# Rank counts, PSUM copies and planner constants of a fused attention and expert kernel

## Chip, cores and metric

One core of a Trainium2 chip runs the whole kernel in one launch. The metric is the time of the execution in device microseconds; the runs shown are medians, and lower is better. The profiled execution is one more execution of the same program.

## The reference, cut to what matters

Capped attention for 8 batches, 12 heads, 448 positions and 64 features per head, then a mixture of 8 experts over all 3,584 tokens, where each expert keeps the 80 tokens with the largest gate weight:

```python
scores = cap * np.tanh((q @ k.T / 8) / cap)
attn = softmax(scores)
x = (attn @ v)                                   # 3584 tokens x 768
logits = x @ w_gate                              # 3584 x 8
expert_idx = argmax(logits, axis=1)
gate_w = softmax(logits)[arange, expert_idx]
for e in range(8):
    tok_idx = tokens of expert e, at most 80, largest gate_w first
    h = relu(x[tok_idx] @ w1[e])                 # 768 -> 1024
    out[tok_idx] = gate_w[tok_idx] * (h @ w2[e]) # 1024 -> 768
```

## The kernel before, in words

**Two stages on one queue of TensorE.** The attention stage runs from the start to about 413 us, the expert stage from there to the end. Everything is float32 and laid out on each engine in an order written by hand.

**The attention stage** goes over 48 pairs of heads (six to a batch), numbered t. One step t issues, in an order written out in the loop at L1341, letters for pieces of work: `q0` to `q3` (products of queries and keys for pair t, each followed by ScalarE's tanh), `x` and `y` (ScalarE's exponentials of pair t and of pair t-1), `a0` to `a2` and `a3` (products of the exponentials with the values for pair t-2), `r` and `s` (GpSimd's partial sums), `u` (on odd t: TensorE sums the exponentials, `SUMS(u)` below, and VectorE transposes and inverts the sums), `n` and `m` (VectorE scales the two products of one pair of pairs, `x(u,0)` and `x(u,1)`, and transposes them). Even t run `q0 q1 y m a0 a1 b q2 q3 s r b x a2 b u`, odd t run `q0 q1 y a0 b q2 q3 a3 u n b x a1 a2 b`. GpSimd adds up the exponentials (L1103, L1105).

After `SUMS(u)` VectorE has a fixed piece of work: `st` (L1124, a transposition of the sums out of PSUM), reciprocals, `r`, the product `x(u,0)` (L1148), its transposition, and the same for the second half. `x(u,0)` has to be done before `a0` of the next even step may write its PSUM bank again, `x(u,1)` before `a0` of the odd step after it.

**The places.** The letter `b` is a place where other work is put in. There are three in a step; below, 24.1 is the second place of step 24. At each, `background` (L1263) takes pieces from three lists: `urgent` (the routing arithmetic of a batch that is just finished), `low` (fetching rows) and `bg` (the ranking). A piece is a cost in nanoseconds, a function that issues its instructions, and a gap: a piece with gap g goes no earlier than g places after the piece taken last from the same list. A place takes pieces until their costs pass a quota, and each cost is added to a planned clock of VectorE that moves on by `PLACE` = 2,630 ns at each place. From step 33 (`LATER`) a piece also has to end within `SLACK` of that clock, a number by parity of t and place. So costs, gaps and slack alone set the order of the instructions on every queue.

**What a batch b brings.** When its six pairs are done (steps 8, 14, ... 44, and the end for b = 7) `gate` queues: `product` (logits into PSUM, `lgp`, L1180), `kept` (the logits copied to SBUF, `lgs`, L1192), `turn` (TensorE transposes them, `lt`, L1199), `math` and the key (some 20 small instructions of VectorE, which end in the sort key `kc`, L327), and `later`, which puts the ranking of the batch's 448 tokens into `bg`: `ranks` (L396). Batches 0 to 4 form the first table, batches 5 to 7 are ranked with its kept entries.

**Ranking.** `row` transposes the keys into PSUM (`psk`) and copies them to SBUF as one row (`krow`); `ties` compares them with themselves (four small tests, L418); `before(c)` compares the whole row so far with the keys of column c (L439, passes of up to 896 columns); `after(c)` lets TensorE count those comparisons (`pd`, L446); `add(c)` adds the counts to `dfc` (L454). Two columns are compared ahead of the count of the first.

**The first table.** After batch 4 `prune` (L544) works out the kept tokens: `order` (o0 to o5 below), `ranked`, `places`, `parts`, `left` (three passes, L586), `right`, `kept`, then `put`, a product of 20 small matmuls (`prt`, L602), and `keys` from it. Its rows are fetched from DRAM ahead of the expert stage.

**PSUM.** All the small results (`sp` of the sums, `psk`, `lgp`, `lt`, `pd`, `prt`) share two banks under the tag `misc`.

**The expert stage** multiplies six tables of 80 rows with their experts' weights (L798); its queue of TensorE follows that of attention, with two chunks started in step 48. The ranking of the last batch goes on beside it.

Of the kernel before, what the change touches and what calls it, by code (L numbers as in the profile page):

```python
# [12 lines left out]
ALU = mybir.AluOpType  # L13
# [4 lines left out]
B, H, S, D = 8, 12, 448, 64  # L18
NP = H // 2
NQ = H // 4  # L20
C = 112
# [3 lines left out]
NC = S // C  # L25
# [11 lines left out]
OB = 5  # L37
# [15 lines left out]
FLIGHT = 5  # L53
PLACE = 2630
LATER = OB * NP + 3
SLACK = ((6500, 6000, 4500), (3000, 6500, 7500))
LATE = 3
RMB = 34
NBUF = 5
# [56 lines left out]
def attn_moe(ctx, tc, q2, k, v, cap, wg, w1, w2, capacity, ct, out):  # L116
    nc = tc.nc
# [25 lines left out]
    def cst(key, n=128):  # L143
        a, b = CT[key]
        return ctt[:n, a:b]
# [15 lines left out]
    acc = consts.tile([C, OCOL, NACC], F32, name="acc")  # L161
# [234 lines left out]
    def ranks(krow, gp, pl, tag, b, acc, dfc, x0, c0, blocks, gw=GW, end=None, ahead_=False):  # L396


        nb = b * NC - c0
        nk = len(blocks)  # L400
        starts = blocks + [x0 + i * C for i in range(nb + NC)]
        PW = PCOL * C

        def row():
            psk = pl.tile([128, 512], F32, name=f"psk{b}", tag=tag, bufs=2)
            for c in range(NC):
                nc.tensor.transpose(psk[:C, c * C:(c + 1) * C], kc[:, b * NC + c:b * NC + c + 1].broadcast_to([C, C]), cst("ident", C)[:, :C])
            z["row"] = nc.scalar.copy(krow[:, x0 + nb * C:x0 + (nb + NC) * C], psk[:C, :S])
            z["psk"] = psk
            held[0] += ahead_  # L410

        gs, z = {}, {}

        def ties():
            held[0] -= 1
            for i, (c, kp, _) in enumerate(cols):
                g = gp.tile([C, C], BF16, name=f"gl{b}_{c}", tag="gl")
                d = nc.vector.scalar_tensor_tensor(g, z["psk"][:C, i * C:(i + 1) * C], kp, cst("tri", C), op0=ALU.is_equal,  # L418
                                                   op1=ALU.mult, accum_out=acc[:, nk + c, 1:2])
                if i == 0:  # L420
                    tc.add_manual_dep(d.ins, z["row"].ins.name, flight, reason="row")

        def tied(c, kp):
            g = gp.tile([C, C], BF16, name=f"gl{b}_{c}", tag="gl")
            x = x0 + c * C
            nc.vector.scalar_tensor_tensor(g, krow[:, x:x + C], kp, cst("tri", C), op0=ALU.is_equal,
                                           op1=ALU.mult, accum_out=acc[:, nk + c, 1:2])

        def before(c, i, x, y, kp, act=False):
            if c not in gs:  # L430
                gs[c] = gp.tile([C, gw], BF16, name=f"gb{b}_{c}", tag="gb", bufs=LATE)
            g, a = gs[c][:, x:y], acc[:, nk + c, 2 + i:3 + i]
            if act:
                nc.vector.tensor_scalar(g, krow[:, x:y], kp, None, op0=ALU.is_ge)
                z = sm.tile([CK, 2, S], F32, name=f"gz{b}_{c}", tag="t1", bufs=4)
                z = z.rearrange("p a b -> p (a b)").bitcast(BF16)[:C, x:y]
                nc.scalar.activation(z, g, AF.Copy, accum_out=a)
            else:
                nc.vector.tensor_scalar(g, krow[:, x:y], kp, 0.0, op0=ALU.is_ge, op1=ALU.add, accum_out=a)  # L439

        def after(c):
            g = gs.pop(c)
            n = nk + c
            pd = pl.tile([128, 512], F32, name=f"pd{b}_{c}", tag=tag, bufs=2)
            for i in range(n):
                nc.tensor.matmul(pd[:, i:i + 1], g[:, starts[i]:starts[i] + 128], ones_b[:, 0:1], start=(i == 0), stop=(i == n - 1))  # L446
            pds[c] = pd[:C, :n]
            held[0] += 1

        def add(c):  # L450
            pd = pds.pop(c)
            held[0] -= 1
            n = pd.shape[-1]
            nc.vector.tensor_tensor(dfc[:, :n], dfc[:, :n], pd, op=ALU.add)  # L454
        pds = {}
        yield 300, row, 2
        cols = [(c, kc[:, c0 + c:c0 + c + 1], x0 + (c + 1) * C) for c in range(nb, nb + NC)]
        if end is not None:
            x = x0 + nb * C

            def first(i):
                c, kp, _ = cols[i]
                return 1700, lambda: before(c, 0, 0, x, kp), 0

            def second(i):
                c, kp, m = cols[i]
                yield 400, lambda: before(c, 1, x, m, kp), 0
                yield 400, lambda: tied(c, kp), 0
            for i in range(LATE):
                yield first(i)  # L470
            for i in range(0, NC, 2):
                yield from second(i)
                yield from second(i + 1)
                yield 100, lambda i=i: after(nb + i), 2
                yield 100, lambda i=i: after(nb + i + 1), 0
                if i == 0:
                    yield first(LATE)
                    yield 200, lambda: add(nb), 0
                    yield 200, lambda: add(nb + 1), 0
                else:  # L480
                    yield 200, lambda i=i: add(nb + i), 1
            yield 800, lambda: end(pds.pop(nb + NC - 1)), 0
            return
        late = []
        gap = 1
        if ahead_:
            yield 1500, ties, 1
            gap = 0
        for c, kp, m in cols:
            for i in range((m + PW - 1) // PW):  # L490
                x, y = i * PW, min(m, (i + 1) * PW)
                yield (y - x) * 1.2 + 120, lambda c=c, i=i, x=x, y=y, kp=kp: before(c, i, x, y, kp), gap
                gap = 0
            if not ahead_:
                yield 400, lambda c=c, kp=kp: tied(c, kp), 0
            if nk + c:
                late.append(c)
            if len(late) == LATE - 1:
                c_ = late.pop(0)
                yield 200, lambda c=c_: after(c), 0  # L500
                yield 200, lambda c=c_: add(c), 1
        for i, c in enumerate(late):
            yield 200, lambda c=c: after(c), int(i == 0)
        for i, c in enumerate(late):
            yield 200, lambda c=c: add(c), int(i == 0)
# [38 lines left out]
    def prune(krow, sm, pl, tag):  # L544

        z = {}
# [122 lines left out]
        for i in range((OCOL + 11) // 12):  # L669
            yield 1000 if i == 0 else 500, lambda i=i: right(i), 0  # L670
        yield 1000, kept, 0
        yield 300, put, 1
        yield 1000, keys, 1
        yield 700, early, 0
        yield 900, rows_in, 0
# [88 lines left out]
    flight = mybir.DependencyInfo(mybir.DependencyClass.Sync, mybir.DependencyReason.DATA)  # L764
# [235 lines left out]
    krow = kr.tile([C, max(OCOL * C, CAND + WCOL * C)], F32, name="krow")  # L1000
# [3 lines left out]
    urgent = []  # L1004
# [6 lines left out]
    st = {"laid": set()}  # L1011
# [4 lines left out]
    with ExitStack() as a2:  # L1016
# [165 lines left out]
        def gate(b):  # L1182
# [6 lines left out]

            def kept():  # L1190
                held[0] -= 1
                nc.scalar.copy(st["lgs", b], st["lp", b][0:96, :S])  # L1192

            def turn():
                lg = st["lgs", b]
# [51 lines left out]
            st["wait"]()  # L1247
            urgent.append((300, product, 0 if b < OB else 1))
            if b < B - 1:
                urgent.append((100, kept, 1))  # L1250
            urgent.append((300, turn, 1 if b < B - 1 else 2))
            urgent.append((1900, lambda: (math(), st["math"][0]()), 1 if b < OB else "ordered"))
            if b < B - 1:
# [9 lines left out]
        def background(quota, took=PLACE, slack=1e9):  # L1263

            now[0] += 1
            clock[0] += took
            for q, last in ((urgent, 1), (low, 3), (bg, 2)):  # L1270
                while q and quota > 0:
                    cost, f, gap = q[0]
                    if gap == "end":
                        if not st.get("end") and quota < 1e8:
                            break
                        gap = 0
                    if gap == "ordered":
                        if not st.get("ordered"):
                            break
                        gap = 1  # L1280
                    if quota < 1e8:
                        if now[0] < now[last] + gap or (gap and slack < 1e8 and clock[0] < ready_at[last]):
                            break
                        if max(clock) + cost > clock[0] + slack:
                            return
                    q.pop(0)
                    quota -= cost
                    vector(cost)
                    now[last] = now[0]
                    ready_at[last] = clock[1]  # L1290
                    f()
# [33 lines left out]
        for t in range(n + 2):  # L1325
# [12 lines left out]
            if 1:  # L1338
# [3 lines left out]
                for i, x in enumerate(todo):  # L1342
# [26 lines left out]
                    elif k_ == 'b' and t < n + 2:  # L1369
                        share = sum(c for c, _, _ in bg + urgent) / (3 * (left - 1) + todo[i:].count('b'))  # L1370
                        share += sum(c for c, _, _ in low) / max(1, 3 * (n - 2 - t))
                        background(min(max(share, 600), 2200 if t < LATER else 3000 if t < n else 4500), PLACE, SLACK[t % 2][todo[:i].count('b')] if LATER <= t < n - 1 else 1e9)
                    if k_ == "b" and t == n + 1 and todo[:i].count("b") == 1:
# [140 lines left out]
```

## Time and profile before

| | us |
|---|---|
| median of 3 runs (lowest, highest) | 529.76 (528.90, 529.96) |
| the profiled execution | 529.38 |
| its span, first to last instruction | 527.2 |
| outside the span | 2.2 |
| attention, 0 to 413.5: TensorE busy, granted clock | 374.3, 0.97 |
| experts, 413.5 to 527.2: TensorE busy, granted clock | 93.9, 0.97 |

A row of the profile names the line, the engine (PE is TensorE, PEld its weight loads, DVE VectorE, ACT ScalarE, POOL GpSimd), the tile written and the tiles read, the shape, a count, and in brackets the idle time ahead of the instruction with what ended it. The granted clock is the share of full speed that TensorE was given: 1.00 is 2.4 GHz and 0.50 is 1.2 GHz.

### The profile page before, as it was taken

The numbers are of one execution on the slowest core, as the hardware profiler recorded it, in microseconds if no ns is written. First come the engines' busy times: TensorE is split into PE (matmuls) and PEld (weight loads), VectorE is DVE, ScalarE is ACT, GpSimd is POOL, SyncE is SP. The second block draws the span as 40 slices with busy tenths as digits, with TensorE's granted clock in tenths as the row PEclk, the third lists the DMA queues.
The fourth block names the chain that finished last, engine by engine and source line by source line (L and its number), as shares of the span: only waits on it lengthen the run. The fifth ranks groups of instructions, "written<-read, shape, count | busy, mean of one in ns | idle before, by whom it ended". The sixth has DMA issues, their size and how long they took to land.

```text
span 527.2 us, 12171 instructions
## 1 busy us (share of the span) xinstructions
PE 468.2 (89%) x4708; PEld 217.0 (41%) x4708; DVE 274.2 (52%) x875; ACT 323.7 (61%) x326; POOL 318.8 (60%) x243
## 2 busy tenths in 40 slices
PE   6799999799999989989999799959978888788894
PEld 2232232223333333323333233323333687787894
DVE  1044435445663585667468955994667835141200
ACT  4988879578888877887888569818850102101111
POOL 0788897587998787799778444624593025325101
PEclk9999999899999999999999899969997999989998
DMA  4675286465576384476674289836356599999901
GB/s 122 193 224 136 67 202 162 119 171 132 146 240 147 77 241 108 107 200 188 137 198 131 67 224 262 204 94 157 80 189 256 170 357 375 387 371 384 360 18 45
DMA packets 82354, 98.15 MB, mean 186 GB/s; under 512 B 37904, under 2 KB 67376, under 8 KB 82288
## 3 DMA queue, kind: packets, MB, share of 16 engines
q1 hardware_dynamic: 80304, 92.66, 60.1%
q0 software_dynamic: 1984, 4.63, 2.7%
q8 instruction: 39, 0.64, 0.5%
q14 instruction: 27, 0.22, 0.1%
HBM read 73.75 MB, written 23.51 MB: 184 GB/s over the span
## 4 chain that ended last, share of the span: by engine, by line
PE 65%; ACT 14%; DVE 13%; issue 6%; DMA 1%; SPq 0%; POOL 0%; POOLq 0%; ACTq 0%; DVEq 0%
PE sc L1061 17%; PE av L1086 13%; PE yt L798 8%; ACT e L1069 8%; PE hp L798 7%; ACT e L1074 5%; PE sp L1119 5%; PE sc L1068 4%; PE av L1095 3%; PE lgp L1180 3%; DVE r L1141 2%; DVE gb L439 2%; PE pd L446 2%; DVE x L1148 2%; DVE rd L1140 1%
## 5 line engine op out<-in xcount | busy, mean ns | idle before, releaser
L1069 ACT ACTIVATE e<-sc,scl 128x896 f32<-128x896 f32 x168 | 162.2, 1014 | 76.6 <-PE sc L1061 70.3
L1074 ACT ACTIVATE e<-e,capt 128x1792 f32<-128x1792 f32 x96 | 154.6, 1611 | 0.0
L1061 PE MATMUL sc<-qt,kt 64*128 64x448 f32 x576 | 140.1, 588 | 10.7 <-ACT e L1069 6.0
L1105 POOL TENSOR_TENSOR t<-t,e 128x896 f32<-128x896 f32 x48 | 100.4, 2092 | 72.1 <-ACT e L1074 70.7
L1086 PE MATMUL av<-e,vr 128*64 128x448 f32 x576 | 134.7, 576 | 2.8 <-issue 2.8
L1103 POOL TENSOR_TENSOR t<-e 128x896 f32<-128x896 f32 x48 | 101.3, 2110 | 34.2 <-ACT e L1074 29.8
L1061 PEld LDWEIGHTS sc<-qt,kt 64*128 64x128 f32 x576 | 49.9, 191 | 83.9 <-ACT e L1069 36.5
L1112 POOL TENSOR_TENSOR t<-t,e 64x448 f32<-64x448 f32 x68 | 76.2, 1130 | 2.6
L1124 DVE STREAM_TRANSPOSE st<-sp 128x448 f32<-128x448 f32 x24 | 15.6, 649 | 110.5 <-PE sp L1119 91.9
L1086 PEld LDWEIGHTS av<-e,vr 128*64 128x64 f32 x576 | 34.3, 139 | 85.2 <-issue 69.9
L439 DVE TENSOR_SCALAR_CACHE_REDUCE gb<-krow,kc 112x896 bf16<-112x896 f32 (+16 forms) x59 | 53.2, 931 | 8.9 <-PE pd L446 8.9
L798 PE MATMUL yt<-thv,w 128*64 128x80 f32 x1152 | 45.1, 238 | 9.7 <-issue 9.7
L798 PEld LDWEIGHTS yt<-thv,w 128*64 128x64 f32 x1152 | 42.9, 141 | 11.2 <-issue 11.1
L798 PE MATMUL hp<-xt,w 128*64 128x80 f32 x1152 | 43.8, 234 | 1.9 <-issue 1.8
L798 PEld LDWEIGHTS hp<-xt,w 128*64 128x64 f32 x1152 | 41.5, 137 | 4.3 <-issue 4.0
L842 POOL DMA_INDIRECT out_dram<-ysv,si x6 | 5.7, 956 | 44.1 <-ACT ysv L841 38.4
L1141 DVE STREAM_TRANSPOSE r<-rd 128x448 f32<-128x448 f32 x48 | 31.0, 645 | 1.7
L1156 DVE STREAM_TRANSPOSE xb<-x 128x448 f32<-128x448 f32 x48 | 30.8, 644 | 1.6
L1148 DVE TENSOR_TENSOR x<-av,r 128x448 f32<-128x448 f32 x48 | 29.8, 620 | 2.1 <-DVE r L1141 0.5
L1119 PE MATMUL sp<-t,ones 128*32 128x448 f32 x192 | 27.9, 568 | 0.8 <-DVE dfc L454 0.8
L814 ACT COPY ty0v<-yt 128x240 f32<-128x240 f32 x6 | 2.2, 359 | 37.6 <-PE yt L798 37.6
L446 PE MATMUL pd<-ones_b,gb 112*128 112x1 bf16 x352 | 13.6, 164 | 12.4 <-DVE gb L439 9.4
(223 smaller groups left out, 341.9 us busy)
## 6 DMA issues: line engine op xcount, KB each, us to landing
w<-in_w_dram SPq DMA_DIRECT2D x36, 512.0 KB, 6.1
w<-in_w_dram SPq DMA_DIRECT2D x48, 384.0 KB, 6.1
kt<-in_k_dram SPq DMA_DIRECT2D x96, 112.0 KB, 2.7
qt<-in_q_dram SPq DMA_DIRECT2D x96, 112.0 KB, 2.9
xs<-xb SPq DMA_DIRECT2D x56, 168.0 KB, 3.5
vr<-in_v_dram SPq DMA_DIRECT2D x24, 256.0 KB, 3.4
out_dram<-zero SPq DMA_DIRECT2D x4, 1536.0 KB, 7.2
vr<-in_v_dram SPq DMA_DIRECT2D x24, 192.0 KB, 3.0
```

What stands on the lines that cost most here:

```text
L439: nc.vector.tensor_scalar(g, krow[:, x:y], kp, 0.0, op0=ALU.is_ge, op1=ALU.add, accum_out=a)
L798: nc.tensor.matmul(ps[j // per][64 * h:64 * h + 64, j % per * m:(j % per + 1) * m], w[:, 128 * j + 64 * h:128 * j + 64 * h + 64], x[:, xk, ...
L1061: nc.tensor.matmul(ps[:, h, :S], s["k"][w, x:x + CK], s["q"][w], start=True, stop=True)
L1069: nc.scalar.activation(s["e"][:, 2 * c:2 * c + 2], ps[:, :, :S], AF.Tanh, scale=scl)
L1074: nc.scalar.activation(x, x, AF.Exp, scale=capt)
L1086: nc.tensor.matmul(st["av", u, f][64 * h:64 * h + 64, :S], st[p]["v"][:, h, c], st[p]["e"][:, 2 * c + h], start=(c == 0), stop=(c == NK - ...
L1103: nc.gpsimd.tensor_tensor(t1, e[:, 0:2], e[:, 2:4], op=ALU.add)
L1105: nc.gpsimd.tensor_tensor(s["es"], s["es"], e[:, 4:6], op=ALU.add)
L1112: nc.gpsimd.tensor_tensor(t1[w, h], t1[w, h], late(p)[w], op=ALU.add)
L1119: nc.tensor.matmul(sp[32 * i:32 * i + 32, :S], ones[:, 0:32], s["es"][:, g % 2, :], start=True, stop=2 * u < RMB)
L1141: nc.vector.transpose(r.rearrange("p (a b) -> p a b", b=32), rd.rearrange("p (a b) -> p a b", b=1).broadcast_to([128, NB, 32]))
L1148: nc.vector.tensor_tensor(x, st["av", u, f][:, :S], st["r", u, f], op=ALU.mult)
```

## The change

Five edits. The copy `krow` of the keys' row is issued by VectorE, at the head of `ties`, where it was ScalarE's in `row` (batch 7 keeps ScalarE's). The copy `lgs` of the logits is VectorE's for batches 0 to 6. `after(c)` gets gap 1 for batches 0 to 3 (gap 0 stays for 4 to 6). `put` gets gap 2. And the planner's numbers change: all six slacks are 1,000 ns larger; a comparison is entered at 1.05 ns a column and 100 ns (1.2 and 120 before), a count at 100 ns (200), `ties` at 1,900 ns (1,500), `kept` at 700 ns (100).

```diff
--- before.py
+++ after.py
@@ -53,7 +53,7 @@
 FLIGHT = 5
 PLACE = 2630
 LATER = OB * NP + 3
-SLACK = ((6500, 6000, 4500), (3000, 6500, 7500))
+SLACK = ((7500, 7000, 5500), (4000, 7500, 8500))
 LATE = 3
 RMB = 34
 NBUF = 5
@@ -405,20 +405,20 @@
             psk = pl.tile([128, 512], F32, name=f"psk{b}", tag=tag, bufs=2)
             for c in range(NC):
                 nc.tensor.transpose(psk[:C, c * C:(c + 1) * C], kc[:, b * NC + c:b * NC + c + 1].broadcast_to([C, C]), cst("ident", C)[:, :C])
-            z["row"] = nc.scalar.copy(krow[:, x0 + nb * C:x0 + (nb + NC) * C], psk[:C, :S])
             z["psk"] = psk
+            if not ahead_:
+                nc.scalar.copy(krow[:, x0 + nb * C:x0 + (nb + NC) * C], psk[:C, :S])
             held[0] += ahead_
 
         gs, z = {}, {}
 
         def ties():
             held[0] -= 1
+            nc.vector.tensor_copy(krow[:, x0 + nb * C:x0 + (nb + NC) * C], z["psk"][:C, :S])
             for i, (c, kp, _) in enumerate(cols):
                 g = gp.tile([C, C], BF16, name=f"gl{b}_{c}", tag="gl")
-                d = nc.vector.scalar_tensor_tensor(g, z["psk"][:C, i * C:(i + 1) * C], kp, cst("tri", C), op0=ALU.is_equal,
-                                                   op1=ALU.mult, accum_out=acc[:, nk + c, 1:2])
-                if i == 0:
-                    tc.add_manual_dep(d.ins, z["row"].ins.name, flight, reason="row")
+                nc.vector.scalar_tensor_tensor(g, z["psk"][:C, i * C:(i + 1) * C], kp, cst("tri", C), op0=ALU.is_equal,
+                                               op1=ALU.mult, accum_out=acc[:, nk + c, 1:2])
 
         def tied(c, kp):
             g = gp.tile([C, C], BF16, name=f"gl{b}_{c}", tag="gl")
@@ -484,12 +484,12 @@
         late = []
         gap = 1
         if ahead_:
-            yield 1500, ties, 1
+            yield 1900, ties, 1
             gap = 0
         for c, kp, m in cols:
             for i in range((m + PW - 1) // PW):
                 x, y = i * PW, min(m, (i + 1) * PW)
-                yield (y - x) * 1.2 + 120, lambda c=c, i=i, x=x, y=y, kp=kp: before(c, i, x, y, kp), gap
+                yield (y - x) * 1.05 + 100, lambda c=c, i=i, x=x, y=y, kp=kp: before(c, i, x, y, kp), gap
                 gap = 0
             if not ahead_:
                 yield 400, lambda c=c, kp=kp: tied(c, kp), 0
@@ -497,7 +497,7 @@
                 late.append(c)
             if len(late) == LATE - 1:
                 c_ = late.pop(0)
-                yield 200, lambda c=c_: after(c), 0
+                yield 100, lambda c=c_: after(c), int(b < OB - 1)
                 yield 200, lambda c=c_: add(c), 1
         for i, c in enumerate(late):
             yield 200, lambda c=c: after(c), int(i == 0)
@@ -669,7 +669,7 @@
         for i in range((OCOL + 11) // 12):
             yield 1000 if i == 0 else 500, lambda i=i: right(i), 0
         yield 1000, kept, 0
-        yield 300, put, 1
+        yield 300, put, 2
         yield 1000, keys, 1
         yield 700, early, 0
         yield 900, rows_in, 0
@@ -1189,7 +1189,7 @@
 
             def kept():
                 held[0] -= 1
-                nc.scalar.copy(st["lgs", b], st["lp", b][0:96, :S])
+                (nc.vector.tensor_copy if b < B - 1 else nc.scalar.copy)(st["lgs", b], st["lp", b][0:96, :S])
 
             def turn():
                 lg = st["lgs", b]
@@ -1247,7 +1247,7 @@
             st["wait"]()
             urgent.append((300, product, 0 if b < OB else 1))
             if b < B - 1:
-                urgent.append((100, kept, 1))
+                urgent.append((700, kept, 1))
             urgent.append((300, turn, 1 if b < B - 1 else 2))
             urgent.append((1900, lambda: (math(), st["math"][0]()), 1 if b < OB else "ordered"))
             if b < B - 1:
```

## Rows read from the trace of the kernel before

**Rows 1.** The page's busy time of each engine over the span

```profile
PE 468.2 (89%) x4708; PEld 217.0 (41%) x4708; DVE 274.2 (52%) x875; ACT 323.7 (61%) x326; POOL 318.8 (60%) x243
```

**Rows 2.** Waits of PE over the run: us in total, times, longest us

```profile
PE pd L446 <- DVE gb L439: 9.4, 7, 4.1
PE prt L602 <- DVE prrh L596: 6.1, 1, 6.1
...
PE lt L1199 <- ACT lgs L1192: 3.3, 6, 0.6
PE av L1086 <- issue: 2.8, 1, 2.8
PE pd L446 <- DVE dfc L454: 2.2, 1, 2.2
PE lgp L1180 <- DVE x L1148: 1.9, 1, 1.9
...
PE sp L1119 <- DVE dfc L454: 0.8, 1, 0.8
PE psk L407 <- DVE st L1124: 0.8, 1, 0.8
```

**Rows 3.** Windows: PE, PEld, DVE, ACT, POOL busy (instructions), granted clock, DMA share, GB/s

```profile
231.10:236.20 5.10, 4.98 (x24) 1.56 (x24) 4.75 (x14) 3.74 (x4) 5.02 (x3) 1.00 0.91 278
319.60:326.00 6.40, 5.83 (x47) 2.21 (x47) 4.42 (x23) 6.28 (x7) 4.17 (x2) 1.00 0.94 241
346.20:356.40 10.20, 7.01 (x34) 3.56 (x35) 9.62 (x24) 0.18 (x1) 0.93 (x1) 0.50 0.26 70
397.40:404.20 6.80, 5.96 (x34) 1.50 (x34) 3.31 (x12) 0.00 (x0) 3.05 (x4) 0.50 1.01 389
```

**Rows 4.** Groups by shape: busy us, mean ns of one, idle before

```profile
L1148 DVE TENSOR_TENSOR x<-av,r 128x448 f32<-128x448 f32 x48 | 29.8, 620 | 2.1 <-DVE r L1141 0.5
L439 DVE TENSOR_SCALAR_CACHE_REDUCE gb<-krow,kc 112x896 bf16<-112x896 f32 x25 | 28.0, 1133 | 0.0
L418 DVE SCALAR_TENSOR_TENSOR gl<-psk,kc,ctt 112x112 bf16<-112x112 f32 x28 | 7.6, 325 | 4.2 <-ACT krow L408 4.2
L1192 ACT COPY lgs<-lgp 96x448 f32<-96x448 f32 x8 | 4.2, 519 | 21.5 <-PE lgp L1180 21.5
```

**Rows 5.** Timeline of PE, 85 to 87 us: start us, us, engine, line, tile

```profile
86.06 1.02 PE L1061 MATMUL sc<-qt,kt 64*128 64x448 f32 x4 [0.27 <-ACT e L1069]
```

**Rows 6.** Waits of PE, 188 to 195 us

```profile
PE pd L446 <- DVE gb L439: 1.5, 2, 1.2
```

**Rows 7.** Waits of PE, 236 to 239 us

```profile
PE pd L446 <- DVE gb L439: 1.6, 2, 1.2
```

**Rows 8.** Timeline of PE and of DVE, 284 to 288 us

```profile
284.04 0.97 PE L1086 MATMUL av<-e,vr 128*64 128x448 f32 x4
...
287.21 0.29 DVE L439 TENSOR_SCALAR_CACHE_REDUCE gb<-krow,kc 112x112 bf16<-112x112 f32 x1
```

**Rows 9.** Timeline of DVE, POOL and PE, 335 to 351 us

```profile
335.67 2.05 DVE L516 TENSOR_TENSOR omo<-neso,ctt 112x64 f32<-112x64 f32 x1
...
344.25 4.16 DVE L586 TENSOR_TENSOR prlh<-r,ctt 112x768 bf16<-112x768 f32 x3
...
350.51 0.64 DVE L1124 STREAM_TRANSPOSE st<-sp 128x448 f32<-128x448 f32 x1
...
335.55 2.09 POOL L1105 TENSOR_TENSOR t<-t,e 128x896 f32<-128x896 f32 x1 [3.80 <-ACT e L1074]
...
342.32 0.95 PE L1121 MATMUL sp<-e,half 128*32 128x448 f32 x8
```

**Rows 10.** Waits of PE, 386 to 414 us; timeline of DVE, 403 to 412

```profile
PE pd L446 <- DVE gb L439: 1.3, 1, 1.3
...
403.49 0.65 DVE L1124 STREAM_TRANSPOSE st<-sp 128x448 f32<-128x448 f32 x1 [3.46 <-PE sp L1121]
...
411.62 0.61 DVE L1148 TENSOR_TENSOR x<-av,r 128x448 f32<-128x448 f32 x1
```

## The prediction

> **What bounds the kernel.** I read the busy times first [rows 1]: TensorE works 89% of the span, no other engine over 61%. Both stages lie on its one queue, so a microsecond taken off anywhere ahead of the last product comes off the end, as long as the late list of rows is still in time. So I read TensorE's waits next [rows 2]. Most name VectorE: counts that wait for their comparisons (9.4 us, seven of them), the first table's product (6.1), the logits' transposition behind ScalarE's copy (3.3, six times 0.6), and smaller ones on `dfc`, `x` and `st`. The 2.8 us put down to "issue" is VectorE too: that product of values waits for `x(17,0)`. Last the clock [rows 3]: around the 6.1 us wait TensorE ran 10.2 us at 0.50 (1.2 GHz), near the end 6.8 us. There a microsecond of work does half a microsecond's worth, so 3.5 us (half of 7.01 busy) and 3.0 us (half of 5.96) were lost beside the waits.
>
> VectorE is in time or late once every two steps. Behind `SUMS(u)` it needs 5.1 us ([rows 3], its stretch from 231.1) for the sums and both halves, and TensorE reaches `a0`, which needs `x(u,0)`, only about 3.5 us behind them (`a1`, `a2`, `q0`, `q1`, each 0.8 to 1.0). So whatever VectorE has left over when the sums are ready comes out as a wait of TensorE of the same length. Between two sums TensorE has 374.3 / 24 = 15.6 us of work (busy time ahead of the experts, in the table above, over 24 pairs of steps).
>
> **Where the pieces go.** Costs, gaps and slacks followed call by call, with the old numbers, give the order that the trace shows; with the new ones: the count of 0.1 (batch 0, column 1) stays at 11.2 and that of 1.0 at 18.0. Batch 2's first count goes from 24.0 to 24.1, its second from 24.2 to 25.1. Batch 3 starts two places later (`row` 29.0, `ties` 29.1) and its first count goes from 30.0 to 30.1. Batch 4's first count, gap still 0, goes forward from 37.0 to 36.2. The chain of the table (`ranked` to `kept`) goes from 42.0 to 43.0 forward to 40.0 to 41.2, `put` from 43.1 to 42.2. Batch 5's ranking runs from 44.1 to 48.2 instead of 47.1 to 49.0, and batch 6's `ties` and first three passes go from 49.2 forward to 49.0, its first count to 49.1.
>
> **The copies.** ScalarE's takes 0.52 us [rows 4]. VectorE's copy of 448 columns out of PSUM isn't in the trace; the same columns out of PSUM with a second operand take it 0.62. I take 0.6, between these ends; 0.1 either way on two pieces doesn't move the sum. *Logits:* VectorE has nothing waiting behind `x` there, and two products of about 1.0 us [rows 5, 8] lie between the logits and their transposition, so the 0.6 us copy is done in time: the six waits go, -3.3. *Keys:* ScalarE's copy stood ahead of a tanh, and TensorE then waited 0.27 us [rows 5], five times alike: -1.4. On VectorE the copy lies ahead of `SUMS`, where it idles; only for batches 3, 4 and 6 does something wait behind it, counted below.
>
> **The counts.** The longest (4.1 us at place 11.2) stands right behind `SUMS(4)` and its 5.1 us, and neither piece moves: nothing. Batch 2 waits 1.5 us [rows 6]; one place on is one product of 1.0 us later, which leaves 0.3: -1.2. Batch 3 waits 1.6 [rows 7]. VectorE has its sums done at 236.2, then now copy 0.6, four tests of 0.33 and passes of 1.13 and (by columns, 560 of 896) 0.71 [rows 4]: comparisons ready at 239.9. TensorE, 1.0 us further on than now, is there at 237.1: a wait of 2.8, +1.2. Batches 3 and 4 also lose where the logits wait for `x`: one pass of 1.1 more stands between the sums and `x(11,1)`, and again `x(14,1)`: +2.2. Batch 4: TensorE is done with `a2` at 285.0, the comparisons of the first count end at 287.5 [rows 8], with the copy 288.1: a new wait of 3.1. It gives VectorE the time that it lacks at `SUMS(17)`, so the 2.8 us there go: +0.3, a stretch at 1.2 GHz in either.
>
> **The table.** Now the chain takes VectorE from 335.67 to 350.51, 14.8 us, and the sums that ended at 343.3 are 7.2 us late [rows 9]. Moved forward, it is cut by `SUMS(19)`: ahead of it lie the 5.1 us behind `SUMS(18)`, the routing arithmetic of batch 5 (4.4 us [rows 3], its stretch from 319.6), two passes for `x(18,1)` (1.3) and the chain up to its first `left` (344.25 - 335.67 = 8.6, and a third of 4.16): 20.8 us against TensorE's 15.6. `SUMS(19)` is 5.2 us late, `a0` waits 4.8. `put` then finds the rest of the chain unfinished by some 1.5 us. With 2.5 us for the clock that is 8.8, against 6.1 + 3.5 = 9.6 now: -0.8. One gap more for the product by itself would only hand the wait on to `a0`.
>
> These 14.8 us hold waits: `omo`, 64 columns, took 2.05 us and ended with GpSimd's addition of 2.09 us that began just ahead of it [rows 9]. The Trainium skill has that rule (GPSIMD Engine Reference, Key points: GpSimd shares its SBUF interfaces with VectorE, and contends with VectorE's instructions that have two SBUF inputs or run in a 2-port mode). The trace agrees, and by it the chain's length depends on where it falls among the additions; that is the second rival.
>
> **The end of attention.** Now it waits 2.2 + 1.9 + 1.3 + 0.8 + 0.8 = 7.0 [rows 2, 10] and loses 3.0 by the clock: 10.0. Batch 5's counts, now spread over steps 45 to 48, keep 1.3 at 46.2 (VectorE 8.5 us behind the sums: 5.1, 2.0 of routing, passes of 1.1 and 0.3; TensorE 7.2: eight groups of four products at some 0.9) and 0.9 at step 48 for the one bank left. But batch 6 now stands ahead of the last `x`. Its count at 49.1 needs 2.5 (first half of the sums' work), copy 0.6, tests 1.3, passes 1.13 and 0.55, 6.1 us behind `SUMS(23)`, where TensorE is after 2.0: a wait of 4.0. `x(23,1)`, 8.1 us behind the sums now [rows 10], comes another 3.2 later (copy 0.6, passes 0.7, 1.1, 0.8), and the logits of batch 7 wait 0.8 for it. With 1.7 for one stretch of 3.4 us at 1.2 GHz: 8.7, -1.3.
>
> **Sum.** -3.3 - 1.4 - 1.2 + 1.2 + 2.2 + 0.3 - 0.8 - 1.3 = -4.3 us. The sum is made against the profiled execution, 529.38 us (span 527.2 and 2.2 outside it, which stay). That is 525.1; the median of the runs shown stands 0.38 higher, so 525.5 beside it. The expert stage I leave as it is: its queue on TensorE is the same.
>
> **Rivals.** *Slower: the clock takes it back.* I count one stretch of about 3.4 us at 1.2 GHz (1.7 us) for a wait of 2.8 to 4.8 us. The two stretches of [rows 3] are 10.2 and 6.8 us long. If each of the four long waits (30.1, 36.2, 42, 49.1) brings 3.4 us more at the lower level than I count, 4 x 1.7 = 6.8 are gone: 532.3. It decides from about 8.6 us of additional time at half clock. For it: after the change there are more long waits than before. Against it: none is as long as 6.1.
> *Faster: the chain slips between GpSimd's additions.* Without 5 of its 14.8 us `SUMS(19)` is in time, `put` too, and all 9.6 go: 516.7. For it: its first small pass takes 2 us now, nearly all of it waiting. Against: GpSimd is busy 60%, and the chain is spread over more additions.
> *No change: the wait only moves.* If the chain is blocked at every addition, `SUMS(19)` is 7 us late, `put` 2.5, and with 3.5 for the clock the table costs 13.0 instead of 9.6: +3.4, and the sum is -0.1: 529.7. The change would then do its copies and nothing with its pacing.
>
> **Numbers.** Forecast 0.57 (its own range 522 to 528), clock 0.15, chain in the gaps 0.14, wait moved 0.14. A measurement here can't tell less than 0.2% (1.1 us) from no change. Faster: most of the forecast and the gaps, 0.67; same: most of the moved wait and a little of the forecast, 0.13; slower: the clock and the rest, 0.20. Forecast 525.5; the range leaves the outer half of the two outer rivals out: 519 to 531.5.
>
> **What would show it.** No `lt <- lgs` wait, and a VectorE copy of 0.6 us ahead of `ties`; no count waiting at 24.0, one of 2.5 to 3 us at 30.1; a new count wait of about 3 us at 36.2 and none at `a0` of 38; `put` waiting under 3 us and `a0` of step 42 some 5; a count at 49.1 waiting 4. The first term to fail would be the table's: a `SUMS(19)` whose `st` starts in time, or 7 us late. The prediction is wrong on the whole if TensorE's time at 0.50 grows by more than 9 us, or if the expert stage, from the last logits on, is longer by more than 2 us: then its list or its weights, not TensorE, set the end.

## The result, and the profile after

The changed kernel takes 522.23 us (median of 4 runs, 520.23 to 523.40), the kernel before 529.33 in the runs beside it: a ratio of 0.9861, 95% interval 0.9828 to 0.9894, 7.1 us. Ratios, here and below, leave out the executions that lie more than 1.5% above the fastest of their kernel. The prediction was 525.5 (519 to 531.5). The profiled execution, 523.40 us with a span of 521.2, is 6.0 below that of before, where the sum said 4.3.

The page of the changed kernel, busy time of each engine (answers to [rows 1]):

```profile
PE 469.6 (90%) x4708; PEld 217.5 (42%) x4708; DVE 280.0 (54%) x889; ACT 317.5 (61%) x312; POOL 318.1 (61%) x243
```

VectorE has 14 copies more and is busy 5.8 us longer in all, ScalarE has 14 fewer and is busy 6.2 us less; TensorE's work is the same. The waits of TensorE over the run (us in total, times, longest; answers to [rows 2]):

```profile
PE pd L446 <- DVE gb L439: 14.4, 11, 4.1
...
PE lgp L1180 <- DVE x L1148: 1.4, 2, 0.9
...
PE pd L446 <- DVE dfc L454: 0.9, 2, 0.6
```

No `lt` waits for `lgs` any more and `prt` doesn't wait at all; the counts wait 14.4 us in place of 9.4. The same in TensorE's timeline (start, us, engine, line, tile, and what it waited for):

```profile
94.98 0.18 PE L446 MATMUL pd<-ones_b,gb 112*128 112x1 bf16 x1 [4.11 <-DVE gb L439]
...
236.95 0.33 PE L446 MATMUL pd<-ones_b,gb 112*128 112x1 bf16 x7 [1.81 <-DVE gb L439]
237.67 0.28 PE L446 MATMUL pd<-ones_b,gb 112*128 112x1 bf16 x5 [0.39 <-DVE gb L439]
...
285.10 0.33 PE L446 MATMUL pd<-ones_b,gb 112*128 112x1 bf16 x7 [0.58 <-DVE gb L439]
286.17 0.35 PE L446 MATMUL pd<-ones_b,gb 112*128 112x1 bf16 x8 [0.74 <-DVE gb L439]
287.61 0.18 PE L446 MATMUL pd<-ones_b,gb 112*128 112x1 bf16 x1 [1.09 <-DVE gb L439]
...
336.68 3.26 PE L1086 MATMUL av<-e,vr 128*64 128x448 f32 x8 [4.33 <-issue]
...
383.84 0.98 PE L1119 MATMUL sp<-t,ones 128*32 128x448 f32 x8 [1.64 <-DVE g L338]
...
401.43 0.40 PE L446 MATMUL pd<-ones_b,gb 112*128 112x1 bf16 x9 [3.30 <-DVE gb L439]
```

These are the counts at 11.2, 30.1 and 36.2, the product of values of step 42, `SUMS(22)` and batch 6's count at 49.1. The windows of half clock ahead of the expert stage (answer to [rows 3]; those of before are the two there and 3.4 us each near 97 and 298; in the expert stage either kernel has one of 3.4 us, near 452 and 469, and one of 6 to 7 us at the very end):

```profile
93.50:100.30 6.80, 5.32 (x15) 2.27 (x17) 3.68 (x13) 2.75 (x3) 0.95 (x1) 0.50 0.60 160
288.10:291.50 3.40, 3.40 (x10) 1.31 (x8) 3.23 (x14) 1.54 (x2) 0.36 (x1) 0.50 0.00 0
335.90:342.70 6.80, 6.02 (x16) 1.67 (x16) 6.48 (x18) 0.92 (x2) 1.64 (x1) 0.50 0.83 215
400.70:407.50 6.80, 5.88 (x59) 3.36 (x61) 6.72 (x19) 0.00 (x0) 0.00 (x0) 0.50 0.27 102
```

Where the time went is read best from one mark in each pair of steps: the start of VectorE's `st` behind each `SUMS(u)`, called u below. The table gives, for each stretch between marks, how much longer it is than in the profiled execution before (us), beside the terms of the prediction that fall into it. "Again" is a second trace of the changed kernel, from the last group of runs below; its last row is left empty, because that group has no trace of the kernel before.

| stretch | predicted | after | again |
|---|---|---|---|
| to u = 4 | -0.8 (logits, keys) | -0.7 | -0.65 |
| to u = 5 | 0 | +0.84 | +0.01 |
| to u = 10 | -1.7 (2 logits, 2 keys) | -1.4 | -1.4 |
| to u = 11 | -1.2 (batch 2) | -1.4 | -1.35 |
| to u = 13 | +0.3 (logits, keys, `x`) | +0.7 | +0.7 |
| to u = 16 | +1.75 (batch 3, `x`, logits) | +1.4 | +1.4 |
| to u = 18 | +0.3 (batch 4) | +1.0 | +0.9 |
| to u = 21 | -1.35 (table, logits) | -2.6 | -2.8 |
| to the last `lt` | -1.6 (end, keys) | -1.4 | +0.3 |
| expert stage | 0 | -2.6 | |

### The profile page after: what moved, and what is told of

Same layout as the page of the kernel before. It is cut to its first block, busy times and chain, and to the rows that moved or that the text cites. A ratio compares the mean times of both kernels' runs of the same rounds, so it can differ in the third digit from the quotient of the medians.

```text
span 521.2 us, 12166 instructions
## 1 busy us (share of the span) xinstructions
PE 469.6 (90%) x4708; PEld 217.5 (42%) x4708; DVE 280.0 (54%) x889; ACT 317.5 (61%) x312; POOL 318.1 (61%) x243
## 4 chain that ended last, share of the span: by engine, by line
PE 70%; DVE 15%; ACT 7%; issue 5%; DMA 1%; POOL 0%; SPq 0%; POOLq 0%; DVEq 0%; ACTq 0%
PE sc L1061 19%; PE av L1086 15%; PE yt L798 8%; PE hp L798 8%; PE sp L1119 5%; ACT e L1069 4%; PE sc L1068 4%; PE av L1095 3%; ACT e L1074 3%; PE lgp L1180 2%; DVE gb L439 2%; DVE r L1141 2%; DVE rd L1140 2%; PE pd L446 2%; DVE x L1148 2%
## 5 line engine op out<-in xcount | busy, mean ns | idle before, releaser
L1061 PE MATMUL sc<-qt,kt 64*128 64x448 f32 x576 | 142.2, 596 | 9.5 <-ACT e L1069 4.8
L798 PE MATMUL yt<-thv,w 128*64 128x80 f32 x1152 | 43.6, 235 | 6.4 <-issue 6.4
L798 PE MATMUL hp<-xt,w 128*64 128x80 f32 x1152 | 46.0, 240 | 2.7 <-issue 2.7
L798 PEld LDWEIGHTS hp<-xt,w 128*64 128x64 f32 x1152 | 43.6, 142 | 4.7 <-issue 4.5
L798 PEld LDWEIGHTS yt<-thv,w 128*64 128x64 f32 x1152 | 41.5, 138 | 7.8 <-issue 7.0
L1119 PE MATMUL sp<-t,ones 128*32 128x448 f32 x192 | 29.1, 551 | 2.0 <-DVE g L338 1.6
L446 PE MATMUL pd<-ones_b,gb 112*128 112x1 bf16 x352 | 13.9, 164 | 15.6 <-DVE gb L439 14.4
L446 PEld LDWEIGHTS <-gb 112*128 112x128 bf16 x352 | 11.5, 97 | 33.8 <-DVE gb L439 20.8
```

The costliest lines, as they stand in the source:

```text
L798: nc.tensor.matmul(ps[j // per][64 * h:64 * h + 64, j % per * m:(j % per + 1) * m], w[:, 128 * j + 64 * h:128 * j + 64 * h + 64], x[:, xk, ...
L1061: nc.tensor.matmul(ps[:, h, :S], s["k"][w, x:x + CK], s["q"][w], start=True, stop=True)
L1119: nc.tensor.matmul(sp[32 * i:32 * i + 32, :S], ones[:, 0:32], s["es"][:, g % 2, :], start=True, stop=2 * u < RMB)
```

## The experiments

The runs were made in three groups of four, and the kernel before was timed again beside each (539.1, 528.7 and 540.2 us: the groups differ by 2%; in the traces most of it lies in the expert stage, which took 117 to 121 us in the first group and 111.3 in before's trace). Ratios are to those. Stretches of a trace are set against the one trace of the kernel before, each sum against the one ahead of it and lengths "up to the last `lt`" from u = 0 on; in the attention they repeat to 0.02 us wherever the clock is the same, which is why single microseconds can be read there.

### The four parts alone

**Logits' copy** on VectorE, at its old place and cost:

```diff
-                nc.scalar.copy(st["lgs", b], st["lp", b][0:96, :S])
+                (nc.vector.tensor_copy if b < B - 1 else nc.scalar.copy)(st["lgs", b], st["lp", b][0:96, :S])
```

> The kernel before, with only the copy of the logits (batches 0 to 6) on VectorE; nothing is moved in the queue. Prediction's term: the six waits of the logits' transposition go, -3.3 us, a ratio of 0.9938 (-4.1 us and 0.992 if each is worth the 0.69 us by which the sums of steps 3, 6 and 9 came earlier in the changed kernel). Rival: VectorE's copy delays x or the sums wait for GpSimd anyway, so that half or more is given back: -1.5 to 0 us, 0.997 to 1.000. In the trace: no wait of lt for lgs; the sums of 3, 6 and 9 about 0.7 us earlier each under the first.

Measured: 0.9908 (0.9879 to 0.9937). The sums of u = 3, 6, 9 and 12 came 0.68 to 0.69 us earlier each, u = 15 0.23, u = 21 about 0.6 (1.9, of which 1.3 are taken for the clock, as in the next run, where nothing was edited there): 3.6 us. The ratio says 3.4 to 6.5. VectorE's copy takes 0.62 us, and nothing behind it gave a part back. The term stands.

**Keys' copy** on VectorE, ahead of the tests:

```diff
-            z["row"] = nc.scalar.copy(krow[:, x0 + nb * C:x0 + (nb + NC) * C], psk[:C, :S])
             z["psk"] = psk
...
+            nc.vector.tensor_copy(krow[:, x0 + nb * C:x0 + (nb + NC) * C], z["psk"][:C, :S])
```

> The kernel before, with only the copy of the transposed keys (batches 0 to 6) on VectorE, ahead of the tests, at the old cost in the plan. Prediction's term: five waits of TensorE behind a delayed tanh go, -1.4 us, ratio 0.9974. Rival, read from the changed kernel's trace: the scores come 0.27 us earlier, and the sums of the same step then wait as much longer for GpSimd's last addition, which does not move: 0 us, 1.000 (up to +0.5 us, 1.001, from the copies that stand ahead of x in batches 4 and 6). In the trace the second wants the gap of 0.27 ahead of the scores gone and the eight products of sp spread over about 0.35 us more.

Measured: 1.0024 (0.9990 to 1.0057), and the sums of u = 4, 7, 10 and 13 within 0.02 us of where they were; at the fifth place, u = 22 came 0.16 us earlier. The term of -1.4 us is next to nothing. Why is seen at the first of the five places. First the kernel before, behind the scores of [rows 5], TensorE's sums and GpSimd's additions ahead of them:

```profile
88.68 1.25 PE L1119 MATMUL sp<-t,ones 128*32 128x448 f32 x8
...
84.31 4.63 POOL L1112 TENSOR_TENSOR t<-t,e 64x448 f32<-64x448 f32 x4
```

then this kernel:

```profile
86.01 1.02 PE L1061 MATMUL sc<-qt,kt 64*128 64x448 f32 x4
...
88.63 1.59 PE L1119 MATMUL sp<-t,ones 128*32 128x448 f32 x8
...
84.59 4.62 POOL L1112 TENSOR_TENSOR t<-t,e 64x448 f32<-64x448 f32 x4
```

The scores no longer wait (0.27 us), and the eight products of `sp`, which began as much earlier against GpSimd's, take 1.59 in place of 1.25 us. They read what GpSimd's fourth addition leaves, and that ends at 89.2, with no gap ahead of it that the copy could close (before: 88.9, 0.27 earlier, like the whole trace). The 0.27 us was a wait ahead of a later wait.

**Counts** one place behind:

```diff
-                yield 200, lambda c=c_: after(c), 0
+                yield 200, lambda c=c_: after(c), int(b < OB - 1)
```

> The kernel before, with only the counts one place behind their comparisons (batches 0 to 3). With the old costs the count of column 1 of batch 0 then moves from 11.2 to 12.0 as well (in the changed kernel it stayed at 11.2), batch 2's first from 24.0 to 24.1, and steps 25 and 31 hold two comparisons of 896 columns ahead of an x. If a wait goes wherever the count has another two products of values ahead of it: -4.1 us and 1.7 us of half clock at 12.0, -1.2 us at 24.1, +1.4 us where the logits of batches 3 and 4 wait for x: -5.6 us, ratio 0.9894. Rival: the comparisons were only hidden by the wait, which turns up at the next sums or at the logits: 0 us, 1.000.

Measured: 0.9896 (0.9860 to 0.9931). u = 5 came 5.14 us earlier (the wait at the count of 0.1 falls from 4.1 to 0.76 us, and no stretch at half clock follows), u = 11 1.37 earlier; then u = 12 and 13 gave 1.3 back and u = 15 1.2, where the logits of batches 3 and 4 wait for `x`:

```profile
95.56 0.18 PE L446 MATMUL pd<-ones_b,gb 112*128 112x1 bf16 x1 [0.76 <-DVE gb L439]
```

So batch 2's place is a loan, paid back within two pairs of steps; batch 0's is a gain. In the whole change that gain isn't there: its lower cost of a comparison lets the count of 0.1 stand at 11.2 again.

**The table's product** one place later:

```diff
-        yield 300, put, 1
+        yield 300, put, 2
```

> The kernel before, with only the first table's product one place later (43.1 to 43.2). Prediction: the wait of 6.1 us is handed on to the next first scores, which need an x that is as late: -1 to +1 us, ratio 0.998 to 1.002. Rival: the product's wait was its own; it goes, and with it the half clock around it: -6 to -9.6 us, 0.982 to 0.989.

Measured: 0.9968 (0.9937 to 0.9998). The wait is still there, shorter by the products of values that now run in it, and the next ones, which need the late `x`, don't wait:

```profile
343.35 1.72 PE L1086 MATMUL av<-e,vr 128*64 128x448 f32 x8
349.54 1.54 PE L602 MATMUL prt<-prrh,prlh 112*96 112x40 bf16 x20 [4.46 <-DVE prrh L596]
...
354.31 2.85 PE L1086 MATMUL av<-e,vr 128*64 128x448 f32 x8
...
353.09 0.63 DVE L1148 TENSOR_TENSOR x<-av,r 128x448 f32<-128x448 f32 x1
```

The sums of u = 20 stand to 0.01 us where they were, those of u = 21 come 1.7 us earlier, as much as the wait is shorter (6.12 to 4.46). How much of this is the edit's depends on the trace that it is set against. Behind the wait TensorE worked 6.8 us at half clock here and 7.0 in before's trace, so against that one all 1.7 us are the edit's. In the run with the keys' copy alone the wait was 6.1 us as before, but only 4.3 us of work fell into half clock, and u = 21 came 1.3 us earlier with nothing edited there; against that one 0.4 us are left. So the edit is worth 0.4 to 1.7 us. That the wait would only be handed on to `a0`, as the prediction says, isn't seen: at half clock TensorE got to `a0` 0.6 us behind the late `x`. A gain of 6 us and more, the rival's, is out.

**Pacing** alone:

```diff
-SLACK = ((6500, 6000, 4500), (3000, 6500, 7500))
+SLACK = ((7500, 7000, 5500), (4000, 7500, 8500))
...
-                yield (y - x) * 1.2 + 120, ...
+                yield (y - x) * 1.05 + 100, ...
...
-                yield 200, lambda c=c_: after(c), 0
+                yield 100, lambda c=c_: after(c), 0
```

> The kernel before, with only the looser pacing: the three slacks 1000 higher, the comparisons at 1.05 a column and 100, a count at 100 in the plan. The chain of the table moves to 40.0 to 41.2 and its product to 42.2, batch 4's first count to 36.2, batch 6's first count to 49.1; the counts of batches 0 to 3 and both copies stay. Prediction's terms: table -0.8, end of attention -1.3, batch 4 +0.3, so -1.8 us, ratio 0.9966. Reading of the changed kernel's trace: from the sums of step 18 to the last transposition of logits about -3.4 us, of which 1.3 is one stretch of half clock less and not the pacing's, and -1 to -2.5 in the expert stage: -3.5 us, 0.9935. Rival: without the copies and the gaps the waits only change place: 0 to +2 us, 1.000 to 1.004.

The new costs of `ties` and `kept` belong to the copies and are left out here. Measured: 0.9915 (0.9884 to 0.9947), 4.5 us; the rival falls. Up to the last `lt` its trace is only 1.0 us shorter (2.7 at the table, 0.8 at the end, less 1.3 for a stretch of half clock at u = 5 that is 6.8 us long in place of 3.4, and less 1.2 at batches 3 and 4). The expert stage, from there on, took 106.9 us, against 111.3 in before's trace; what that is worth is taken up below.

### What the parts do together

**The changed kernel with the keys' copy back on ScalarE** (that edit undone, all else as changed):

> The changed kernel, with the copy of the transposed keys back on ScalarE. Prediction's term: +1.4 us on the changed kernel, 0.9861 becomes 0.989, and the sums of steps 4, 7 and 10 come 0.27 us later each. Rival (the sums wait for GpSimd's last addition either way): 0 us, 0.986, and these sums where they are in the changed kernel, to 0.02 us.

Measured: 0.9847 (0.9805 to 0.9888), against 0.9861 for the changed kernel, and the sums of u = 4, 7 and 10 where they were. The copy doesn't even come free: u = 14 is 0.54 us and u = 17 0.58 us earlier without it. There VectorE's comparisons are what TensorE's count waits for, and the copy (0.58 us) stands ahead of them.

**The changed kernel with batch 0's counts two places behind**, so that 0.1 gets to 12.0:

```diff
-                yield 100, lambda c=c_: after(c), int(b < OB - 1)
+                yield 100, lambda c=c_: after(c), (1 + (b == 0)) * (b < OB - 1)
```

> The changed kernel, with batch 0's counts two places behind their comparisons in place of one, so that column 1's goes from 11.2 to 12.0, the place that the gap alone gave it. If the changed kernel's lower cost of a comparison in the plan undid the gap at this place: the 4.1 us wait and its half clock go, the sums of step 5 come 5.1 us earlier (as with the gap alone) and nothing behind takes it back: -5 us on the changed kernel, ratio 0.977. Rival: with the logits' copy on VectorE ahead of it the wait turns up at step 6 or at the next count: -2 to 0 us, 0.982 to 0.986.

Measured: 0.9818 (0.9788 to 0.9847). u = 5 came 5.14 us earlier, as with the gap alone, so the two parts of the change did work against each other at 11.2. But by the ratios it is 2.3 us ahead of the changed kernel, not 5, and the two intervals overlap. In the profiled execution 3.0 us go at u = 14: the wait at 30.1 is the same 1.81 us, and now a stretch of half clock follows that the changed kernel didn't have, which may be chance (see the last section). Its timeline and its window there:

```profile
230.27 0.33 PE L446 MATMUL pd<-ones_b,gb 112*128 112x1 bf16 x7 [1.81 <-DVE gb L439]
```

```profile
230.60:237.40 6.80, 6.41 (x21) 1.98 (x21) 5.47 (x13) 2.90 (x4) 6.65 (x6) 0.51 0.66 165
```

**The change without its pacing** (both copies, the gap, the product, at the old costs and slacks):

> The kernel before, with both copies on VectorE, the counts one place behind and the table's product one place later, at the old costs and slacks: the change without its pacing. If the parts measured alone add up: -3.6 (logits), 0 (keys), -4.1 (counts), -0.4 (product), so -8.1 us up to the last transposition of logits and 0.985 or less; then the pacing, which takes 12.0 back to 11.2, is worth nothing in the whole change. Rival: the pacing carries the gain of the table and the end, and without it the sum is the prediction's -4.3 less 1.8, with half of the gap's gain lost to x: -3 us, 0.994.

Measured: 0.9818 (0.9790 to 0.9845). Up to the last `lt` it is 9.0 us shorter than before, with 5.14 at u = 5 among them. The parts add up to about that (3.6, 4.1 and 0.4 to 1.7), but chance is in it too: behind the table's wait TensorE worked 3.4 us at half clock here, 7.0 in before's trace. So up to there the changed kernel, which has the pacing, is 5.6 us slower than this one (3.4 us shorter than before, not 9.0). The place u = 5 alone makes 6.0 of that (5.14 earlier here, 0.84 later there): the pacing takes 12.0 back to 11.2. If it is worth something, then in the expert stage: 111.5 us here, against 106.4 to 106.9 in the three kernels with the pacing in this group.

### Towards a better version, and the changed kernel once more

**Keys on ScalarE and batch 0's counts two places behind**, the first two edits of the section above together (and the cost of `ties` back at 1500):

> The changed kernel, with the keys' copy back on ScalarE (and its old place cost) and batch 0's counts two places behind. If the keys' copy on VectorE buys nothing and stands ahead of the counts of batches 3 and 4 and of the last one, and the two edits add up: the sums of step 5 come 5.1 us and those of steps 14 and 17 another 0.5 us each earlier than in the changed kernel, -6 us on it, ratio 0.975. Rival: the copy was no cost, the 0.5 us were the clock's: -5 us, and the time of the changed kernel with batch 0's counts alone moved, 0.982.

Measured: 0.9674 (0.9644 to 0.9705), against 0.9829 (0.9778 to 0.9880) for the changed kernel in this group. That is 8.4 us; the medians of the executions that the ratios use, 523.0 and 528.7, say 5.7. Up to the last `lt` it is 10.9 us shorter than before, where the changed kernel's two traces have 3.4 and 2.8. The two profiled executions of this group are only 0.4 us apart (525.70 and 526.12), because this one's expert stage took 118.3 us and the other's 110.7.

**Batch 3 two places earlier as well**, by the logits' copy at its old cost:

```diff
-                urgent.append((700, kept, 1))
+                urgent.append((100, kept, 1))
```

> The kernel of the run before this one, with the logits' copy at its old cost of 100 in the plan (it stays on VectorE), so that batch 3 starts two places earlier and its first count stays at 30.1. If the wait at 30.1 (1.8 and 0.4 us in the changed kernel) is the late start of batch 3 alone: it goes, the logits of batch 4 wait about 0.9 us as before or 0.8 less, -2 to -3 us, ratio 0.970. Rival: the comparisons then stand ahead of x at steps 29 and 30, and a product of values waits for as long: 0 us.

Measured: 0.9664 (0.9614 to 0.9715), not to be told from the run before. The wait at 30.1, 1.27 and 0.39 us in the run before, fell to 0.25 and 0.39, and the stretch from u = 13 to 16 is 2.5 us shorter. Of these, 1.65 us are the clock's: the run before had 3.4 us of half clock there, and the changed kernel with its keys on ScalarE, with the same wait of 1.27 us, had none. The old cost also moves batch 5's counts back, and TensorE waits there:

```profile
379.91 0.40 PE L446 MATMUL pd<-ones_b,gb 112*128 112x1 bf16 x10 [2.20 <-DVE dfc L454]
...
389.09 0.98 PE L1119 MATMUL sp<-t,ones 128*32 128x448 f32 x8 [2.10 <-DVE dfc L454]
```

From u = 21 to the last `lt` it lost 3.7 us on the run before, with 10.2 us of half clock in place of 6.8.

**Batch 6's first count a place later on top of that**:

```diff
-                yield 100, lambda c=c_: after(c), (1 + (b == 0)) * (b < OB - 1)
+                yield 100, lambda c=c_: after(c), (2, 1, 1, 1, 0, 0, 1, 0)[b]
```

> The kernel of the run before this one, with batch 6's counts one place behind too, the first from 49.1 to 49.2. If the 3.3 us wait there is only VectorE's lateness, two products of values more (1.7 us) halve it: -1.7 us up to the last transposition of logits, and up to 1 us of half clock. Rival: the logits of batch 7 wait for x, which is as late, or the expert stage, paced by its weight transfers, gives it back: 0 us, and the later counts of batch 6 lengthen the expert stage by 1 us.

Measured: 0.9692 (0.9647 to 0.9738), no gain. The count waits 2.77 us at its new place, against 1.51 at 49.1 in the run before; from u = 21 to the last `lt` the two differ by 0.4 us.

**The changed kernel again**:

> The changed kernel again, on the chip of the three others: ratio 0.9861 (0.983 to 0.989). A second trace of one program: what differs between the two stretches at half clock, in places where the work is the same, is chance, and is no part of the change. If the sums of step 5 stand at +0.84 and those of step 21 at -2.72 against the step before once more, both are the change's; if they differ by about 1.3 us with one stretch of 3.4 us more or less, they are the clock's.

Measured: 0.9829 (0.9778 to 0.9880). u = 5 stands at +0.01, and the stretch of half clock there is 3.4 us:

```profile
95.60:99.00 3.40, 3.40 (x12) 1.32 (x10) 1.69 (x5) 1.84 (x2) 0.00 (x0) 0.52 0.59 169
```

So the +0.84 of the first trace was the clock's, and the -2.7 us from u = 20 to 21 repeat. The last stretch doesn't (+0.3 against -1.4): TensorE worked 8.5 us at half clock there, in stretches of 6.8 and 3.4 us, against 5.9 in the first trace, which makes 1.3 of the 1.7 us.

## Why the prediction held, and where it didn't

The frame held: TensorE's one queue sets the attention, and VectorE's lateness comes out of it as waits. The time lies in the forecast's own range of 522 to 528, near its lower end, and that is in part luck. All terms of the sum lie in the attention, and there the changed kernel is 3.4 us shorter in the first trace and 2.8 in the second, where the sum says 4.3; the rest of the 6.0 us between the profiled executions came in the expert stage, which the sum left as it was. By its steps:

- **Logits, -3.3:** 3.6 us alone. Right. (The six waits are five of 0.62 us and one of 0.16, not six times 0.6; the sum of 3.3 is as said.)
- **Keys, -1.4:** the step that failed. It took a 0.27 us wait ahead of the scores for time, without asking what the sums behind them wait for. They wait for GpSimd's last addition. Measured 0 at four of the five places and 0.16 at the fifth. What the copy costs in batches 3 and 4, 1.1 us, stands in the prediction's terms for them.
- **Counts of batches 2 and 3 and the `x` of the logits, -1.2, +1.2, +2.2:** -1.4 at u = 11; 1.8 + 0.4 of waiting at 30.1 (said: 2.8); about 1.4 up to u = 13 and 1 up to u = 16 given back at the logits. Right within 0.6.
- **The count of 0.1, 0:** right as to its place and its 4.1 us. What wasn't seen is that this is where the change loses most, for the gap by itself moves it and gains 5.1.
- **Batch 4, +0.3:** +1.0. The new wait came in three pieces, 2.4 us in all (said: 3.1); half a microsecond is the keys' copy, for without it the stretch takes +0.4 (pacing alone, and the changed kernel with the keys on ScalarE).
- **Table, -0.8:** right in its course, too small against the trace of before. `SUMS(19)` was late and step 42's product of values waited 4.33 us (said: 4.8), with 3.0 lost by the clock (said: 2.5); but `put` didn't wait 1.5, it didn't wait at all. 7.3 in place of 8.8, so -2.3 against the 9.6 of before. Part of the 9.6 was chance: in the runs with one copy alone the same wait of 6.1 us was followed by 4.5 and 4.3 us of work at half clock, not 7.0, which makes 8.3 to 8.4; against these the table gains 1.0 to 1.1. The chain got through partly between GpSimd's additions, the faster rival's mechanism: its three `left` took 2.3 us, against 4.16 in [rows 9]. That one gap more for the product would only hand the wait on isn't borne out either: by itself it was worth 0.4 to 1.7 us.

```profile
332.66 0.95 DVE L586 TENSOR_TENSOR prlh<-r,ctt 112x768 bf16<-112x768 f32 x1
...
338.49 1.39 DVE L586 TENSOR_TENSOR prlh<-r,ctt 112x768 bf16<-112x768 f32 x2
```

- **End of attention, -1.3:** -1.4 in one execution and +0.3 in the other, so its size isn't settled. In the first the waits came nearly as said (1.14 at 46.2, 0.9 at step 48, 3.30 at 49.1, none at the last logits), with one that wasn't: 1.64 us ahead of `SUMS(22)`. Just ahead of it VectorE's 32 columns of `ohv` were caught by a GpSimd addition:

```profile
381.30 1.88 DVE L329 TENSOR_TENSOR ohv<-rev,cmn 112x32 f32<-112x32 f32 x1
...
381.04 2.09 POOL L1105 TENSOR_TENSOR t<-t,e 128x896 f32<-128x896 f32 x1
```

In the second trace the same `ohv` got in 0.02 us ahead of the addition, took 0.18 us, and `SUMS(22)` didn't wait. This is the rule of the Trainium skill (GPSIMD Engine Reference, Key points) that the prediction set beside [rows 9]; the trace agrees, and the price is up to the addition's whole 2.1 us. But nothing was won by it there: `SUMS(23)` waited 2.74 us in place of 0.35, for counts (`dfc`) whose own wait the trace puts down to no engine.

- **Expert stage, 0:** 2.6 us off in the profiled execution. That its queue on TensorE is the same was not reason enough: the pacing moves part of batch 6's ranking out of it (27 of 2344 recorded products, 7 of 112 instructions of VectorE). With the pacing it took 108.7 us in the first trace and 106.9, 106.4 and 106.5 in the second group; without it 111.3 in before's trace and 111.5 in the second group. But in the last group four kernels with the pacing took 110.7 to 118.3, and in the first group four without it, their expert stage alike, 117 to 121. So executions differ by more than that, and how much of the 2.6 is the change's is not settled. Nor is the mechanism: in both profiled executions, before and after, the DMA engines are 94% busy or more there until the last weights are issued, and no run delayed one weight or one count by itself.

Of the rivals, the clock took nothing back: the stretches at half clock ahead of the last one sum to 27.3 us in the traces of before and after, though there are more long waits (30.7 in the second trace of the changed kernel). That the wait only moves is out for the table (7.3, not 13.0). The surplus over the forecast, 6.0 against 4.3 in the profiled execution, is a sum of misses of both signs: +1.4 for the keys, +0.8 of chance at u = 5, +0.7 at batch 4, -1.5 at the table (some 1.3 of it the clock's chance in the trace of before), -2.6 in the expert stage, which make -1.2, and smaller ones.

## What to carry to other kernels

A wait is worth its length only if nothing later in the same step waits for another engine anyway: before pricing it, look at what the next join reads (here GpSimd's last addition) and when that is ready. Where pieces are placed by their estimated costs, follow each edit through the plan alone and together with the others; here a lower cost undid a gap at the one place where the gap was worth 5 us. Part-by-part runs of a change found a version 6 to 8 us faster than the whole. And a stretch at half clock belongs to the trace that it was read from: set an edit against more than one trace before a microsecond of it is called the edit's.

## What the runs showed of the hardware

The same wait of 4.1 us at the same count (0.1) was followed by 3.4 us at 1.2 GHz in four traces and by 6.8 us in four others, the changed kernel's two among them on either side. u = 5 then stood at 0, +0.01, +0.04 and +0.39 us with the shorter, at +0.58, +0.84, +1.10 and +1.30 with the longer stretch. A wait of 1.8 us at 30.1 had none behind it in two traces and 6.8 us in a third, one of 1.27 us there none in one trace and 3.4 us in another. So a microsecond beside such a wait, read from one trace, says nothing.

A VectorE instruction with two operands in SBUF can be held for the length of a GpSimd addition however small it is: 8 columns (`prx`) took 1.95 us and 20 columns (`us`) 2.00 in the changed kernel, each ending with the addition, against 0.17 to 0.18 for the same instruction when it was not held.
